# An attention + two-MoE kernel: finer pooling sums, a later load of the third batch, and the branch for further items moved between the two MoEs

## Chip, cores and metric

The kernel runs on one core of one Trainium2 chip. The metric is device time in microseconds (us): the median of the runs shown, lower is better. The profile is one more execution of the same program, with its own time.

## What is computed

```python
# attention: q, k, v are (8 batches, 8 heads, 576 rows, 64); K and V are pooled by 8 rows
k_p = k.reshape(B, H, Sp, pool, D).mean(axis=3)      # Sp = 72
v_p = v.reshape(B, H, Sp, pool, D).mean(axis=3)
attn = softmax(scale * q @ k_p.T)                    # 576 x 72 for each head
x = (attn @ v_p), heads side by side                 # 4608 tokens x 512
# first MoE: 8 experts (512 -> 1024 -> 512), each token goes to its best expert only
out[mask] = gate_w[mask, None] * (relu(x[mask] @ w1[e]) @ w2[e])
# second MoE: dense, three 512 -> 768 products, the largest of them, and back to 512
h = max(x @ w1, x @ w2, x @ w3)                      # elementwise
return h @ w_out                                     # 4608 x 512
```

All data are float32; products are made of high and low parts.

## The kernel before

The order of work on each engine is the order in which the code issues it; nothing reorders it. Three stretches follow each other.

**Attention (0 to about 160 us).** A loop over `it` runs 36 tiles of queries, and places beside them loads, pooling and the routing. SyncE (SP) loads: a batch's K and V come with `load_rows` (L193 for the rows of full 128-row chunks, L200 for a rest of 64 rows), a batch's queries with `load_q` (L215, tile `qgrp`). When K and V of batch `kvnext` are asked for is set by one condition in that loop, `kvnext * 4.5 - 11 <= it`; queries are asked for by `qorder` and `qneed`. In one turn of the loop the queries come first in the code, then K and V.

`prep_steps(b)` makes a batch's pooled K and V. For V always (`pool_v`), and for K from the third batch on (`pool_k2`), GpSimd (POOL) sums the 8 rows in three halvings, w = 4, 2 and 1: each `tensor_tensor` adds half of the rows to the other half in place (L267 for K, L280 for V), and the last one writes the pooled row to `kp` or `vp`. A batch has 576 pooled rows (8 heads of 72): four chunks of 128 partitions and one of 64. `spread_v` (L288) then sets V out by heads, also on POOL. VectorE (DVE) meanwhile takes maxima, subtracts (`sh`), normalises (L500 to L517), and works out the tokens' experts and their ranks in them (tiles `lg`, `oh`, `pre`, `im`; helpers at L547 and L551).

**First MoE (about 160 to 701 us).** Tokens are sorted by expert into items of 128. `run(range(NREQ), ...)` does the 22 items that are always needed (18 pairs of items and 4 single ones); the number of single items in fact needed is read from `nsing` (`values_load`, L1555) on all engines, when those 22 are issued. Results go to `ybuf` by SP (L1146). In gaps the weights of the second MoE are combined and written to `wdram` (L1169 to L1245).

**Second MoE (701 to 1246 us), `second`.** 6 groups of 768 tokens; in each, 9 chunks of weights (`wt`, 128x3584, loaded at L1585 into three buffers: the first three by POOL, all others by SP) go through `quad`: 42 matmuls each (L1617). The first 36 matmuls of the second MoE read the first chunk, `wt_0`, and the 37th reads `wt_1`. The products of seven sub-blocks are put together by ScalarE (ACT, `s`, L1625) and DVE (`blk`, `m`); then the output product (L1693), a copy by ACT with the gate (`ob`, L1699) and an indirect scatter to the output by POOL (`out_rows`, L1700). `tokens(g)` gathers the gates of a group (L1602, POOL). The rows of the first group are read from the first MoE's tiles while that MoE still runs.

**The branch.** Should more than 4 single items be needed, a branch (`tc.If(need > NREQ - NPAIR)`, L1757) after the second MoE runs them (`more`), two at a time, and does the last group of `second` once more, since such items hold tokens of that group. For these inputs it isn't taken. Every engine comes to it with its own compare-and-branch; an engine that skips it runs, at the end, instructions that bring the semaphores to where the skipped block would have left them, after a wait for its own earlier work (SP: for the DMAs of its queues, POOL: for those of its own, `INC_SWDGE_SEM` among them). The end of the program follows (L1798: drains and a barrier).

Of the kernel before, what the change touches and what calls it, by code (L numbers as in the profile page):

```python
# [8 lines left out]
F32 = mybir.dt.float32  # L9
# [5 lines left out]
A = mybir.AluOpType  # L15
AX = mybir.AxisListType.X
PSUM = bass.MemoryType.PSUM
# [4 lines left out]
def attention_moe_moe_kernel(  # L22
# [24 lines left out]
    nc = tc.nc  # L47
    dbg = dbg or {}

    P = 128  # L50
    B, H, S, D = q.shape
    N, DM = out.shape
    E, _, F = w1.shape
# [4 lines left out]
    DC = DM // P  # L58
# [4 lines left out]
    NPAIR = 18  # L63
    NSING = 8
    NB = 2 * NPAIR + NSING
    NITEM = NPAIR + NSING
    NREQ = NPAIR + NSING // 2
# [18 lines left out]
    GW = 768  # L86
    HW = GW // 2

    def pool(stack, name, bufs, side="left", space=None):
        kw = {"space": space} if space else {"side": side}  # L90
        return stack.enter_context(tc.tile_pool(name=name, bufs=bufs, reuse_waits="tile", **kw))
# [24 lines left out]
    if True:  # L116
# [61 lines left out]
        if True:  # L178
# [69 lines left out]
            def prep_steps(b):  # L248
# [14 lines left out]
                def pool_k2():  # L263
                    for c0, c1, n in ((0, 4, P), (4, 5, RC[4])):
                        for w in (4, 2, 1):
                            dst = kt[0:n, c0:c1, 0:w, :] if w > 1 else kp[0:n, c0:c1, 0:1, :]
                            nc.gpsimd.tensor_tensor(  # L267
                                dst, kt[0:n, c0:c1, 0:w, :], kt[0:n, c0:c1, w : 2 * w, :], op=A.add
                            )

                def dup_k():
                    for c0, c1, n in ((0, 3, P), (3, 4, KC[3]), (4, 5, KC[4])):
# [1 line left out]

                def pool_v(c0, c1, n):
                    for w in (4, 2, 1):
                        for a0 in range(c0, c1, 2) if w == 4 else (c0,):
                            a1 = min(a0 + 2, c1) if w == 4 else c1
                            dst = vt[0:n, a0:a1, 0:w, :] if w > 1 else vp[0:n, a0:a1, :].unsqueeze(2)
                            nc.gpsimd.tensor_tensor(  # L280
                                dst, vt[0:n, a0:a1, 0:w, :], vt[0:n, a0:a1, w : 2 * w, :], op=A.add
                            )
# [656 lines left out]
            def open_a(stack=left):  # L939

                tl["split"] = pool(stack, "wsplit", 3)
                tl["x"] = pool(stack, "xrow", 2)
# [25 lines left out]
            def load_w(i, piece):  # L968
                if i >= last[0]:
                    return  # L970
                if i >= NE:
                    finish_routing("slots")
                if piece == 0:
                    vals[i] = nc.sync.value_load(etab[0:1, i : i + 1], min_val=0, max_val=E - 1)
                e_ = bass.ds(vals[i], 1)
                if piece < 4:
                    src = w1[e_, :, 256 * piece : 256 * piece + 256].rearrange("o (c p) f -> p (o c) f", p=P)
                else:
                    src = w2[e_, 256 * (piece - 4) : 256 * (piece - 3), :].rearrange("o (c p) d -> p (o c) d", p=P)
                if i in (0, NREQ):  # L980
                    nc.sync.dma_start(w_raw(piece), src)
                else:
                    nc.sync.dma_start(w_raw(piece), src, cond=(vals[i] != vals[i - 1]), bounds_check="skip_entire_dma")
# [287 lines left out]
            def columns(g, whole_=True):  # L1271

                w_ = HW if whole_ else HW // 3
                at_ = [(c, n) for c in range(2) for n in range(0, HW, w_)]
                rows = []

                def load(k_):
                    if k_ < len(at_):
                        c, n = at_[k_]
                        t = tl["yr"].tile([P, 2, 2, w_], F32, tag="yr", name=f"yr{g}_{c}_{n}", bufs=2)
                        src = ybuf[:, GW * g : GW * g + GW].rearrange("(i c p) (j n) -> c p i j n", i=2, c=2, j=2)
                        for i in range(2):
                            nc.sync.dma_start(t[:, i], src[c, :, i, :, n : n + w_])
                        rows.append((t, c, n, w_))

                load(0)  # L1290
                load(1)
                for _ in range(1 if whole_ else 8):
                    yield
                for k_ in range(len(at_)):
                    yield from sums(*rows[k_])
                    load(k_ + 2)
# [180 lines left out]
            for it in range(NT + 4):  # L1477
                boundary()
                if it == MA:
                    skv.close()  # L1480
                    open_a()

                    for c in range(DC):
                        nc.gpsimd.dma_start(
                            ybuf[c * P : (c + 1) * P, N - (NITEM - NREQ) * P : N].rearrange("p (a n) -> p a n", n=P),
                            ones.unsqueeze(1).to_broadcast([P, NITEM - NREQ, P]),
                        )
                if it == NT:
                    sq_.close()
                    open_b()  # L1490
                while qnext < len(qorder) and qorder[qnext][0] * 9 + qneed[qorder[qnext][1]] - 4 <= it:
                    load_q(*qorder[qnext])
                    qnext += 1
                while kvnext < B and kvnext * 4.5 - 11 <= it:
                    kv[kvnext] = (load_rows("kraw", k, kvnext, KC if kvnext < 2 else RC), load_rows("vraw", v, kvnext, RC))
                    kvnext += 1
                if 0 <= it - 1 < NT:
                    stage_s(it - 1)
                if 0 <= it - 3 < NT:
                    stage_a(it - 3)  # L1500
                if it < NT:
                    stage_q(it)
                if 0 <= it - 1 < NT:
                    stage_e(it - 1)
                while squares:
                    squares.pop()()
                if it >= NT + 2:
                    next(first)
                if dense[0] == 2 and it < NT:
                    boundary()  # L1510
                if 0 <= it - 4 < NT:
                    stage_x(it - 4)
                if it == NT + 1:
                    next(first)
                for job in todo.get(it, []):
                    if callable(job):
                        job()
                        continue
                    b, j = job
                    if b not in cur:  # L1520
                        cur[b] = prep_steps(b)
                    cur[b][j]()
                if it == NT - 1 and started:
                    next(first)
                    next(first)
                if it == NT:
                    next(first)
                if it == NT + 3 or it - 3 in [t1 for _, t1 in CHK]:
                    while squares:
                        squares.pop()()  # L1530
                for m, (_, t1) in enumerate(CHK[:-1]):
                    if it - 4 == t1 - 1 and t1 < NT1:
                        queue.append([chain(rank_steps(m), slot_steps(nc.gpsimd))])
                    elif it - 4 == t1 - 1:
                        queue.append([chain(rank_steps(m), early_steps())])
                        dense[0] = 2
# [16 lines left out]
        for _ in cb:  # L1553
            pass
        need = nc.values_load(nsing[0:1, 0:1], min_val=0, max_val=NSING)  # L1555
    left.close()


# [6 lines left out]
    GB = GW // P  # L1565
    CH = F2C // 2 * 3

    def second(st, groups, again=False):
        wq = pool(st, "wstream", 3)
        yp = pool(st, "yin", 2)  # L1570
        t2 = pool(st, "tmp2", 2)
# [137 lines left out]
        for k_ in range(3):  # L1709
            load_chunk(k_)  # L1710
        tokens(groups[0])
        ahead = columns(groups[0]) if again else iter(())
        for g in groups:
            for _ in ahead:
                pass
# [23 lines left out]

    with ExitStack() as st:  # L1740
        second(st, list(range(NG)))

    def more(i0):

        last[0] = i0 + 2
        for p_ in range(8):
            load_w(i0, p_)
        gather(i0)
        for _ in run(range(i0, i0 + 2), lambda half, p_: None):
            pass  # L1750
        if i0 + 2 < NITEM:
            with tc.If(need > i0 + 2 - NPAIR):
                more(i0 + 2)


    assert (NITEM - NREQ) * P <= GW
    with tc.If(need > NREQ - NPAIR):  # L1757
        with ExitStack() as st:
            pq = pool(st, "pq2", 2, space=PSUM)
            pb = pool(st, "pb2", 1, space=PSUM)  # L1760
            wp1 = pool(st, "w1again", 1)
            tl["w1"] = [wp1.tile([P, DC, 256], F32, name=f"w1again{i}") for i in range(4)]
            tl.pop("py")
            open_a(st)
            open_c(st)
            more(NREQ)
        with ExitStack() as st:
            second(st, [NG - 1], True)


# [32 lines left out]
```

## Time and profile before

| | us |
|---|---|
| median of 3 runs | 1263.38 (1262.02 to 1263.81) |
| the profiled execution | 1260.98 |
| its span, first to last instruction | 1259.2 |
| PE busy in the span | 1215.6 (97%) |
| DVE busy | 799.2 (63%) |
| ACT busy | 580.5 (46%) |
| POOL busy | 318.9 (25%) |
| mean granted clock of TensorE | 0.991 of full speed |

The profiled execution lies 2.4 us below the median. A sum of changes is made on it and then set on the median. A line of a timeline reads: start, duration, engine, line, operation, out<-in, and in brackets how long the engine had been idle and what ended it. Lines of a source view read: line, engine, operation, count, durations in ns (minimum, median, maximum), first and last start in us. "SPq", "POOLq", "PEldq" are the sequencers of these engines (branches, semaphores, DMA issues).

### The profile page before, as it was taken

To read this page: it belongs to the slowest core of one execution; us is meant where nothing else is said; L and a number is where in the kernel's file an instruction comes from. 1 tells how busy PE (TensorE), PEld (TensorE's weight loads), DVE (VectorE), ACT (ScalarE), POOL (GpSimd) and SP (SyncE) were. 2 spreads that over 40 slices of the span, in tenths; PEclk is the share of its full clock that TensorE was granted. 3 is DMA by queue.
4 is the path that set the end of the run, shared out by engine and by line. 5 is a ranking of instruction groups with operands and counts; after the bars stand their busy time and mean duration, and the time that the engine had idled before them with its cause. 6 is when DMAs were issued, how large, how long until landed. Compare 5 with 4: busy or idle time off the path is not lost. (4 is left out here: it accounts for less than half of the span.)

```text
span 1259.2 us, 22318 instructions
## 1 busy us (share of the span) xinstructions
PE 1215.6 (97%) x8251; PEld 1158.0 (92%) x8251; DVE 799.2 (63%) x1575; ACT 580.5 (46%) x1040; POOL 318.9 (25%) x383
## 2 busy tenths in 40 slices
PE   5899899999999999999999999999999999999995
PEld 4788789999999999999999998998998998998994
DVE  6676886797889999898764446345445454454450
ACT  3466465545666676666655333323223323223221
POOL 6985553420212212222000302103103004004001
PEclk9899999999999999999999999999999999999998
DMA  9968246423976445844619666475564673773721
GB/s 252 267 202 236 97 138 217 151 85 32 298 262 226 164 143 203 283 151 137 207 51 350 241 238 242 160 262 205 207 239 182 220 264 153 258 263 124 253 108 52
DMA packets 98038, 246.21 MB, mean 196 GB/s; under 512 B 17100, under 2 KB 58106, under 8 KB 89858
## 3 DMA queue, kind: packets, MB, share of 16 engines
q1 hardware_dynamic: 84770, 189.09, 44.5%
q0 software_dynamic: 13152, 55.62, 13.3%
q8 instruction: 67, 1.10, 0.4%
q14 instruction: 49, 0.40, 0.1%
HBM read 252.23 MB, written 46.98 MB: 238 GB/s over the span
## 5 line engine op out<-in xcount | busy, mean ns | idle before, releaser
L1617 PE MATMUL p<-yhi,wt 128*128 128x384 f32 x1512 | 387.2, 336 | 0.0
L1617 PEld LDWEIGHTS p<-yhi,wt 128*128 128x128 f32 x1512 | 273.4, 188 | 0.6
L1617 PE MATMUL p<-ylo,wt 128*128 128x384 f32 x756 | 254.0, 336 | 0.0
L1625 ACT COPY s<-p 128x384 f32<-128x384 f32 x162 | 77.8, 480 | 221.1 <-PE p L1617 216.8
L1104 PE MATMUL py<-hhi,whi 128*128 128x256 f32 x576 | 164.6, 286 | 0.0
L1104 PE MATMUL py<-hhi,wlo 128*128 128x256 f32 x576 | 163.1, 283 | 1.6 <-DVE wlo L1036 1.6
L1056 PE MATMUL ph<-xhi,whi 128*128 128x256 f32 x576 | 163.8, 284 | 0.7 <-DVE hlo L1072 0.7
L1056 PE MATMUL ph<-xhi,wlo 128*128 128x256 f32 x576 | 163.0, 283 | 0.7 <-DVE wlo L1036 0.7
L1056 PE MATMUL ph<-xlo,whi 128*128 128x256 f32 x576 | 163.0, 283 | 0.0
L1104 PE MATMUL py<-hlo,whi 128*128 128x256 f32 x576 | 162.9, 283 | 0.0
L1617 PEld LDWEIGHTS p<-ylo,wt 128*128 128x128 f32 x756 | 142.1, 188 | 0.5
L1646 DVE TENSOR_TENSOR blk<-p,s 128x384 f32<-128x384 f32 x108 | 59.7, 553 | 113.9 <-PE p L1617 113.9
L1602 POOL DMA_INDIRECT gt<-gbuf,ix x26 | 37.0, 1424 | 312.1 <-DMA ix<-idbuf 305.7
L1104 PEld LDWEIGHTS py<-hhi,wlo 128*128 128x128 f32 x576 | 110.4, 192 | 1.8 <-DVE wlo L1036 1.8
L1056 PEld LDWEIGHTS ph<-xhi,whi 128*128 128x128 f32 x576 | 110.5, 192 | 1.2 <-DVE hlo L1072 0.9
L1056 PEld LDWEIGHTS ph<-xhi,wlo 128*128 128x128 f32 x576 | 110.5, 192 | 0.9 <-DVE wlo L1036 0.9
L1056 PEld LDWEIGHTS ph<-xlo,whi 128*128 128x128 f32 x576 | 110.5, 192 | 0.0
L1104 PEld LDWEIGHTS py<-hlo,whi 128*128 128x128 f32 x576 | 110.5, 192 | 0.0
L1104 PEld LDWEIGHTS py<-hhi,whi 128*128 128x128 f32 x576 | 110.4, 192 | 0.0
L1036 DVE TENSOR_TENSOR wlo<-w2raw,whi 128x1024 fp32r<-128x1024 f32 x84 | 102.2, 1221 | 8.8 <-ACT whi L1034 8.7
L1036 DVE TENSOR_TENSOR wlo<-w1raw,whi 128x1024 fp32r<-128x1024 f32 x67 | 81.8, 1220 | 27.6 <-ACT whi L1034 26.5
L1034 ACT CAST whi<-w2raw 128x1024 fp32r<-128x1024 f32 x88 | 91.8, 1044 | 7.7 <-PE py L1104 4.7
(316 smaller groups left out, 2280.8 us busy)
## 6 DMA issues: line engine op xcount, KB each, us to landing
wt<-wdram SPq DMA_DIRECT2D x51, 1792.0 KB
w1raw<-in_moe_w_dram SPq DMA_DIRECT2D x88, 512.0 KB
w2raw<-in_moe_w_dram SPq DMA_DIRECT2D x88, 512.0 KB
wdram<-wst POOLq DMA_DIRECT2D x9, 1792.0 KB
ybuf<-yo SPq DMA_DIRECT2D x40, 256.0 KB
cvraw<-in_moe_w_dram POOLq DMA_DIRECT2D x36, 256.0 KB
vraw<-in_v_dram SPq DMA_DIRECT2D x8, 1024.0 KB
xbuf<-x SPq DMA_DIRECT2D x16, 512.0 KB
```

The source lines that it names most:

```text
L1034: nc.scalar.copy(hi, src)
L1036: eng.tensor_tensor(lo, src, hi.bitcast(F32), op=A.subtract)
L1056: nc.tensor.matmul(ps[:, f, :], a_[:, c, fs], b_[:, c, :], start=(n == 0), stop=(n == 3 * DC - 1))
L1104: nc.tensor.matmul(py[:, c // 2, (c % 2) * 256 : (c % 2 + 1) * 256], a_[:, f, c * P : (c + 1) * P], b_[:, f, :], start=(piece == 0 and f = ...
L1602: nc.gpsimd.indirect_dma_start(out=gt[g][:, j : j + 1], out_offset=None, in_=gbuf[:, :], in_offset=bass.IndirectOffsetOnAxis(ap=cols[j], a ...
L1617: nc.tensor.matmul(ps, a_, b_, start=(start and c + n == 0), stop=(c == 1 and n == 2), skip_group_check=True)
L1625: nc.scalar.copy(t, ps)
L1646: tt(src, add[0], add[1], op=A.add)
```

## The change

Three edits. Line numbers after the first of them shift by up to 18: L1555 becomes L1557, L1585 becomes L1603, L1602 becomes L1620, L1617 becomes L1635.

```diff
 def pool_k2():
     for c0, c1, n in ((0, 4, P), (4, 5, RC[4])):
         for w in (4, 2, 1):
-            dst = kt[0:n, c0:c1, 0:w, :] if w > 1 else kp[0:n, c0:c1, 0:1, :]
-            nc.gpsimd.tensor_tensor(
-                dst, kt[0:n, c0:c1, 0:w, :], kt[0:n, c0:c1, w : 2 * w, :], op=A.add
-            )
+            for a0 in range(c0, c1, 4 // w):
+                a1 = min(a0 + 4 // w, c1)
+                dst = kt[0:n, a0:a1, 0:w, :] if w > 1 else kp[0:n, a0:a1, 0:1, :]
+                nc.gpsimd.tensor_tensor(
+                    dst, kt[0:n, a0:a1, 0:w, :], kt[0:n, a0:a1, w : 2 * w, :], op=A.add
+                )
...
 def pool_v(c0, c1, n):
     for w in (4, 2, 1):
-        for a0 in range(c0, c1, 2) if w == 4 else (c0,):
-            a1 = min(a0 + 2, c1) if w == 4 else c1
+        for a0 in range(c0, c1, 4 // w):
+            a1 = min(a0 + 4 // w, c1)
...
-                while kvnext < B and kvnext * 4.5 - 11 <= it:
+                while kvnext < B and max(kvnext * 4.5 - 11, kvnext - 1) <= it:
...
         need = nc.values_load(nsing[0:1, 0:1], min_val=0, max_val=NSING)
+
+        def more(i0):
+
+            last[0] = i0 + 2
+            for p_ in range(8):
+                load_w(i0, p_)
+            gather(i0)
+            for _ in run(range(i0, i0 + 2), lambda half, p_: None):
+                pass
+            if i0 + 2 < NITEM:
+                with tc.If(need > i0 + 2 - NPAIR):
+                    more(i0 + 2)
+
+
+        with tc.If(need > NREQ - NPAIR):
+            more(NREQ)
     left.close()
...
-    def second(st, groups, again=False):
+    def second(st, groups):
...
-        ahead = columns(groups[0]) if again else iter(())
+        ahead = iter(())
...
     with ExitStack() as st:
         second(st, list(range(NG)))
 
-    def more(i0):
...
-    with tc.If(need > NREQ - NPAIR):
-        with ExitStack() as st:
...
-            more(NREQ)
-        with ExitStack() as st:
-            second(st, [NG - 1], True)
```

**POOL, the pooling of K and V of the third batch.** Names ending in a number are tiles; a shape is the output's, `x4` is a count of equal rows. Before:

```order
L267 TENSOR_TENSOR kraw_254<-kraw_254 128x4x256
L267 TENSOR_TENSOR kraw_254<-kraw_254 128x4x128
L267 TENSOR_TENSOR kp_484<-kraw_254 128x4x64
L267 TENSOR_TENSOR kraw_254<-kraw_254 64x256
L267 TENSOR_TENSOR kraw_254<-kraw_254 64x128
L267 TENSOR_TENSOR kp_484<-kraw_254 64x64
L280 TENSOR_TENSOR vraw_257<-vraw_257 128x2x256 x2
L280 TENSOR_TENSOR vraw_257<-vraw_257 128x4x128
L280 TENSOR_TENSOR kp_484<-vraw_257 128x4x64
```

Now:

```order
L269 TENSOR_TENSOR kraw_287<-kraw_287 128x256 x4
L269 TENSOR_TENSOR kraw_287<-kraw_287 128x2x128 x2
L269 TENSOR_TENSOR kp_490<-kraw_287 128x4x64
L269 TENSOR_TENSOR kraw_287<-kraw_287 64x256
L269 TENSOR_TENSOR kraw_287<-kraw_287 64x128
L269 TENSOR_TENSOR kp_490<-kraw_287 64x64
L282 TENSOR_TENSOR vraw_290<-vraw_290 128x256 x4
L282 TENSOR_TENSOR vraw_290<-vraw_290 128x2x128 x2
L282 TENSOR_TENSOR kp_490<-vraw_290 128x4x64
```

Every sum over 128 partitions now covers 256 elements of each. The first sum with w = 2 reads what the first two sums with w = 4 wrote, with two more of these between; before, it read what the instruction right before it wrote. The two first batches change in V alone.

**SP, the loads after V of the second batch (`vraw_251`, now `vraw_254`).** Before:

```order
L193 DMA kraw_254<-in_k_dram 128x4x512
L200 DMA kraw_254<-in_k_dram 64x512
L193 DMA vraw_257<-in_v_dram 128x4x512
L200 DMA vraw_257<-in_v_dram 64x512
L215 DMA qgrp_2_288<-in_q_dram 128x8x256
```

Now:

```order
L215 DMA qgrp_2_285<-in_q_dram 128x8x256
L193 DMA kraw_287<-in_k_dram 128x4x512
L200 DMA kraw_287<-in_k_dram 64x512
L193 DMA vraw_290<-in_v_dram 128x4x512
L200 DMA vraw_290<-in_v_dram 64x512
```

One load of queries goes ahead of the third batch's K and V; all later batches keep their places.

**POOL, between the MoEs.** In brackets: the semaphores of a row's wait (DMAHW: SP's DMAs, DMASW: POOL's own). Before, from the read of `nsing`:

```order
L1555 TENSOR_LOAD nsing [waits DVE_49]
L1585 DMA wt_0_9369<-wdram_63 128x3584 [waits DMAHW4_49,DMAHW5_49,DMAHW3_49,DMAHW6_49,DMAHW2_49,DMAHW7_49,DMAHW1_49,DMAHW0_49]
L1585 DMA wt_1_9371<-wdram_64 128x3584 [waits DMAHW3_49,DMAHW6_49,DMAHW1_49,PE_49]
L1585 DMA wt_2_9373<-wdram_65 128x3584
```

Now, from the end of the skipped block (the branch itself, L1572, stands right behind the read of `nsing`):

```order
L1568 UNCONDITIONAL_BRANCH
L1572 ISA [waits DMASW6_49,DMASW7_49,DMASW1_49,DMASW0_49]
L1572 UNCONDITIONAL_BRANCH
L1603 DMA wt_0_9987<-wdram_63 128x3584 [waits DMAHW4_49,DMAHW3_49,DMAHW5_49,DMAHW2_49,DMAHW6_49,DMAHW1_49,DMAHW7_49,DMAHW0_49,DMASW6_49]
L1603 DMA wt_1_9989<-wdram_64 128x3584 [waits DMAHW4_49,DMAHW3_49,DMAHW5_49,DMAHW1_49,DMAHW6_49,DMAHW0_49,DMAHW7_49,DMASW7_49,PE_49]
L1603 DMA wt_2_9991<-wdram_65 128x3584 [waits DMASW0_49]
```

The load of `wt_1` waited for three of SP's DMA semaphores and now waits for seven, at values that SP reaches only when it has skipped the block; for `wt_0` the values are ones that SP reaches before it. PE's first matmul of the second MoE follows the branch on its engine, and waits for ACT's skip too:

```order
L1128 MATMUL pyT_9939<-ident,yr_9937 128x128 x4
L1568 UNCONDITIONAL_BRANCH x2
L1572 UNCONDITIONAL_BRANCH
L1635 MATMUL p_0_0_10012<-yhi_8110,wt_0_9987 128x384
L1635 MATMUL p_0_0_10012<-ylo_8111,wt_0_9987 128x384
```

Before, the first `p` matmul (L1617) stood right behind `pyT` and PE's read of `nsing`. At the end of the program POOL's last rows of before, `L1757` branches and an `ISA`, are gone: the end (L1789, before L1798) follows the last scatter.

## Rows read from the trace of the kernel before

**Rows 1.** Page, busy time, share of the span and instructions of each engine.
```profile
PE 1215.6 (97%) x8251; PEld 1158.0 (92%) x8251; DVE 799.2 (63%) x1575; ACT 580.5 (46%) x1040; POOL 318.9 (25%) x383
```

**Rows 2.** Waits of PE, 16 to 150 us: total, times, longest.
```profile
PE pav L490 <- DVE dt L515: 4.6, 2, 3.2
...
PE psc L436 <- DVE pre L547: 2.4, 1, 2.4
```

**Rows 3.** Windows: length, busy of PE, PEld, DVE, ACT, POOL, then clock, DMA share, GB/s.
```profile
40.00:45.00 5.00, 4.31 (x20) 3.63 (x21) 1.47 (x4) 1.99 (x5) 4.76 (x6) 0.69 1.08 281
45.00:50.00 5.00, 5.00 (x26) 4.69 (x24) 2.26 (x5) 2.22 (x5) 4.76 (x6) 0.63 1.07 340
...
130.00:140.00 10.00, 6.84 (x41) 5.99 (x40) 10.00 (x11) 2.52 (x6) 9.61 (x12) 0.83 0.10 34
```

**Rows 4.** Timeline, POOL and DVE, around 35 us and 131 us.
```profile
33.76 4.04 DVE L551 TENSOR_SCALAR im<-iof 128x10 f32<-128x10 f32 x1
...
35.42 3.69 POOL L267 TENSOR_TENSOR kraw<-kraw 128x1024 f32<-128x1024 f32 x2
...
41.48 3.83 POOL L280 TENSOR_TENSOR vraw<-vraw 128x512 f32<-128x512 f32 x3
...
129.57 3.92 DVE L547 TENSOR_TENSOR oh<-w,wm 128x72 f32<-128x72 f32 x1
...
131.06 3.67 POOL L267 TENSOR_TENSOR kraw<-kraw 128x1024 f32<-128x1024 f32 x2
```

**Rows 5.** POOL by line and shape, 0 to 160 us: count, busy us, mean ns.
```profile
L267 POOL TENSOR_TENSOR kraw<-kraw 128x1024 f32<-128x1024 f32 x6 | 14.1, 2351 | 0.0
...
L267 POOL TENSOR_TENSOR kp<-kraw 128x256 f32<-128x256 f32 x6 | 4.4, 730 | 0.7 <-PE ptk L313 0.4
```

**Rows 6.** Timeline, SP and PE, the queries of tile `qgrp`.
```profile
23.59 0.59 SPq L215 DMA_DIRECT2D qgrp<-in_q_dram  x1
...
40.69 0.63 PE L411 MATMUL pqT<-ident,qgrp 128*128 128x128 f32 x4 [2.88 <-DMA qgrp<-in_q_dram]
```

**Rows 7.** Timeline, POOL, between the MoEs.
```profile
658.53 0.58 POOL L1585 DMA_DIRECT2D wt<-wdram  x1
...
695.45 1.08 POOL L1585 DMA_DIRECT2D wt<-wdram  x2 [36.34 <-DMA ybuf<-yo]
...
707.29 1.00 POOL L1602 DMA_INDIRECT gt<-gbuf,idg  x1 [1.30 <-DMA wt<-wdram]
```

**Rows 8.** Timeline, PE, ACT and SP, where the second MoE begins.
```profile
700.79 0.66 PE L1126 MATMUL pyT<-ident,yr 128*128 128x128 f32 x4 [0.68 <-ACT yr L1097]
...
701.33 0.41 PE L1617 MATMUL p<-yhi,wt 128*128 128x384 f32 x1
...
701.48 0.59 ACT L1128 COPY yo<-pyT 128x512 f32<-128x512 f32 x1 [0.74 <-PE pyT L1126]
...
701.76 0.51 PE L1617 MATMUL p<-yhi,wt 128*128 128x384 f32 x2
702.09 0.39 SPq L1146 DMA_DIRECT2D ybuf<-yo  x1
...
702.29 0.51 PE L1617 MATMUL p<-yhi,wt 128*128 128x384 f32 x2
```

**Rows 9.** DMA of 690 to 712 us in 40 slices of 0.55 us, GB/s.
```profile
GB/s 382 377 310 156 76 47 21 5 0 0 0 15 235 182 235 443 417 469 417 417 417 417 443 391 443 469 417 417 426 111 304 86 0 0 1 0 0 31 0 131
```

**Rows 10.** Source view of the branch of before, at the end of the program.
```profile
L1757 SPq EVENT_SEMAPHORE  x9: 17/17/17, 1207.7 to 1208.7; - x9
...
L1757 SPq COMPARE_BRANCH  x1: 53/53/53, 1201.4 to 1201.4; - x1
L1757 DVEq COMPARE_BRANCH  x1: 72/72/72, 1224.8 to 1224.8; - x1
L1757 DVEq EVENT_SEMAPHORE  x1: 21/21/21, 1225.4 to 1225.4; - x1
L1757 PEldq COMPARE_BRANCH  x1: 3372/3372/3372, 1241.6 to 1241.6; - x1
...
L1757 POOLq INC_SWDGE_SEM  x1: 1810/1810/1810, 1249.9 to 1249.9; - x1
```

**Rows 11.** Timeline, POOL, the last scatter.
```profile
1247.03 0.98 POOL L1700 DMA_INDIRECT out_dram<-ob,ix  x1 [2.99 <-ACTq L1757]
```

**Rows 12.** Source view of L1798, the program's end.
```profile
L1798 POOLq DRAIN  x3: 46/109/6689, 1251.7 to 1258.9; - x3
```

More of the change, by code (lines that the diff above doesn't have):

```diff
@@ L1741, in attention_moe_moe_kernel @@
         second(st, list(range(NG)))
-    def more(i0):
[L1745 to L1756, printed above, removed]
-    with tc.If(need > NREQ - NPAIR):
-        with ExitStack() as st:
[L1759 to L1765, printed above, removed]
-            more(NREQ)
-        with ExitStack() as st:
-            second(st, [NG - 1], True)
 _INS = [
```

## The prediction, made before the changed kernel was run

> **What bounds the kernel now.** I read the page first: PE is busy 97% of the span, ACT and DVE about half of it or somewhat more, POOL a quarter [rows 1]. So the time is PE's stream of matmuls, plus the places where that stream stands still or runs at the lower clock, plus the tail after it. Whatever the change does must show in one of these three, and I went to each place that it touches.
>
> In the attention, the waits of PE show that its two long ones behind DVE end at `dt` and `pre` [rows 2]. Both are small DVE operations that wait for POOL. The timeline shows how: `oh`, 72 elements, takes 3.92 us, from 129.57 to about 133.4, and POOL's first K sum runs from 131.06 and takes 2.35 us [rows 4, 5], that is, to 133.4. `im`, 10 elements, takes 4.04 us, from 33.76 to 37.80, and the K sum that starts at 35.42 ends at 37.77. So DVE did not get in where one POOL instruction followed another at once, but where a sum had to wait for the one right before it. The windows add the price behind a wait: after PE's pauses the granted clock is 0.69 and 0.63 over 40 to 50 us and 0.83 over 130 to 140 us; 5 x 0.31 + 5 x 0.37 = 3.4 us are lost in the first of these, 1.7 us in the second [rows 3].
>
> Between the MoEs PE runs on without a wait: `pyT` at 700.79, then the first `p` matmul at 701.33 [rows 8]. At the end, the last scatter is issued at 1247.03 [rows 11], POOL's `INC_SWDGE_SEM` starts at 1249.9 [rows 10] and a drain of 6.69 us at 1251.7 [rows 12].
>
> **The change, part by part.**
>
> *Finer sums.* A sum of 256 elements takes 0.73 us alone [rows 5]; back to back I reckon 0.69. With w = 4 and 2 a batch's K then takes (4 + 2) x 0.69 = 4.14 instead of 3.69 us, its V 4.14 instead of 3.83 [rows 4]: POOL works 0.3 us longer for each of the first two batches, 0.75 for each of six others. Only in the opening does PE wait on a sum itself: +0.3. The rest lies beside PE's work, and POOL's pooling isn't late elsewhere. But the stretch in which DVE is held changes. Before, a gap came after the first K sum, 2.35 us after the start. Now the first sum with w = 2 needs a result two instructions back, so the first gap comes where w = 1 waits for w = 2, after 4.14 us. `oh` would get in at 131.06 + 4.14 = 135.2 instead of 133.4: +1.8 us, and PE, which waits 3.2 us there for the `dt` queued behind `oh` on DVE, waits longer by as much. The pause that ends at `pre` is held by V in the same way, 2.5 us to the first gap before, 4.14 now: +1.6. Some of it comes back, since the later gaps lie closer together, and POOL's added work shifts which DVE operation meets which sum. I take +2 for both with the opening's 0.3. The bounds: if every boundary now lets DVE in, the pauses at `dt` and `pre` go (3.2 + 2.4) with the 1.7 of clock behind the first, -7; if both are fully lengthened and another lock arises, +5.
>
> The Trainium skill ("SBUF — State Buffer", section on who interferes with whom) calls the port pair that DVE and GpSimd share an exclusive lock; read as one lock for each instruction, shorter instructions would let DVE in sooner, and the sum would be negative here. The rows above agree with the lock and speak against release at each boundary: `oh` was queued before 131.06, when POOL's spread ended and K began, and did not get in there.
>
> *Later load of the third batch.* The queries `qgrp` were issued at 23.59 behind K and V of that batch, and PE waited 2.88 us for them, to 40.69 [rows 6]. They now go first, and land earlier by the 2.36 MB that went ahead of them, 7 us or more at 281 to 340 GB/s [rows 3]; that wait goes. What is late next is DVE: `im` would be held to 35.42 + 4.14 = 39.56 instead of 37.80, and the softmax chain behind it on DVE, on which PE's next products stand, slips by 1.8 us. K of that batch lands some 4 us later, which POOL, on V and spreads until 35.4, just covers. I take 0; the bounds are +1.5 and -6.3 (all of 2.88, and 3.4 of clock).
>
> *The branch between the MoEs.* Its code is skipped, but each engine brings its semaphores up after its own work, and POOL's load of `wt_1` now waits for SP's skip. Before, `wt_1` was issued at 695.45 [rows 7], and the first 36 matmuls, 0.52 us for three [rows 8], ended at 701.33 + 6.25 = 707.6, where `wt_1` is first read. Now: SP issues the last `ybuf` store at 702.09, 0.39 us long [rows 8]; it lands about 2 us later (the last scatter: issue ends at 1248.0, landed by 1249.9 [rows 10, 11]), at 704.4. Until then SP reads `nsing` and jumps. Jumps cost, from compare to first semaphore, 0.6 us on DVE, 3.37 on PE for the compare alone, and 6.3 on SP (1201.4 to 1207.7), with nine semaphores over 1.0 us behind it [rows 10]. SP's was behind a chunk of 1.8 MB then in flight and would not be now; I take 2 us from 703.4, so semaphores from 705.4 to 706.1. `wt_1` is issued there. Its flight: both chunks were issued at 695.45 and landed at 707.29, where a gather that waits for them goes [rows 7]; one chunk of 1.835 MB takes 4.3 us at the 430 GB/s shown [rows 9], so the first landed near 703, 7.5 us after its issue. 706.1 + 7.5 = 713.6 against 707.6: **+6.0**. PE's own start (ACT's skip, a jump like the 3.37) moves quad 0 to 702.7 to 705, which this wait hides: 705 + 6.25 = 711.3. `wt_2` and six gathers queue behind `wt_1` on POOL; `wt_2` is needed a quad (7.3 us) later and lands 4.3 later, so it adds nothing. Bounds: +4 (no cost of SP's jump beyond the store, a flight of 6.5) and +10 (a jump of 6.3); 2 us to 3.4 more if the pause drops the clock as it did at 41 and 134 us.
>
> The Trainium skill ("Runtime: NRT & Kernel Launch", section on instruction fetch mechanics) says that a taken branch whose target lies outside the window of loaded pages stalls until the target's page is fetched. PE's 3.37 us agree, DVE's 0.6 us do not show such a stall; by the rule alone, SP's jump would be nearer PE's, and the sum 1.4 us higher.
>
> *The end.* The branches, the wait for the last scatter's landing and `INC_SWDGE_SEM` (1.81 us) go. If the drain of 6.69 us then starts where the last issue ends, 1248.0 instead of 1251.7, the end comes 3.7 us sooner: **-3.7**. Bounds: 0 (the drain is itself the wait for something that ends at its own time), -1.8 (it counts from the landing) and -8 (it only followed from `INC_SWDGE_SEM`, and shrinks as well, to leave only the landing).
>
> **Sum:** +2 + 0 + 6.0 - 3.7 = +4.3 us. On the profiled 1260.98 that is 1265.3; on the median of 1263.38, which I forecast, 1267.7, rounded to **1267**.
>
> **Rivals.**
>
> *A. DVE gets in (faster).* If the finer sums free DVE at each boundary, the pauses behind `oh`, `pre` and `im` and for `qgrp` go: up to -7 and -6.3; half of it, -6.5, with +6.0 and -3.7 gives -4, about 1259; all of it 1253. It decides once the opening and attention give back more than the 2.3 us that the middle and the end leave. For it: each of these pauses is a real pause of PE, and no row of before shows sums as short as these back to back at 128 partitions. Against: the boundaries of equal instructions in rows 4. Chance 0.22.
>
> *B. The end gives more than assumed (faster or even).* The drain shrinks: -8 against +6 and 0 to +2: 1261 to 1263.5. For it: the two other drains take 0.05 and 0.11 us [rows 12]. Against: nothing shows what the long one waits for. Chance 0.13.
>
> *C. Middle and end cancel (even).* SP's jump is hidden by the store and the wait is +4, the attention moves by less than 1: about 1264. Chance 0.15.
>
> *D. Worse.* SP's jump costs 6 us or the clock falls behind the new pause: +9 in the middle, +7 in sum: 1271. Chance 0.15.
>
> The forecast itself has 0.35. That the change doesn't do what it says is no rival: the order shows each row moved, and the branch stays not taken.
>
> **Numbers.** A measurement of this kernel tells about 0.2%, 2.5 us, from no change: faster means under 1260.9, slower over 1265.9. Faster: A's larger part 0.17 and 0.07 of B, with 0.04 from C and the forecast's edge: 0.28. Same: the rest of B, most of C and a part of A and the forecast: 0.22. Slower: 0.50. Range: 1256 (A without its extreme) to 1273 (D with some of the attention's upper bound); the forecast's own cases alone lie at 1264 to 1270.
>
> **What would show it.** `wt_1` issued about 706 and PE waiting for it near 711 to 713, with a `DMA wt<-wdram` wait of 2 to 5 us; no `INC_SWDGE_SEM` at the end and the long drain from 1248 relative to the last scatter; `oh` longer than 3.9 us, `im` longer than 4.0; no `qgrp` wait at 40 us. It is wrong if `wt_1` goes out before 703, if DVE's small operations under POOL's sums fall to under 1.5 us and PE's pauses at 37, 89 and 130 us shrink, or if the drain vanishes.

## The result, and the profile after

The changed kernel takes **1281.82 us** (median; 1280.39 to 1283.68), the kernel before in the same runs 1263.6: ratio 1.0141, 95% interval 1.0118 to 1.0164, 15 to 21 us slower. Forecast: slower, to 1267, in 1256 to 1273. The direction was right, the size was not: the time lies above the range. The profiled execution took 1282.09 us, its span is 1280.4.

I followed PE through both traces: it issues the same 8251 matmuls in the same order, so each can be set against its counterpart. On the clock of the kernel before, the changed kernel's lag is -0.3 us at 25 us, +5.8 at 37, back to +0.7 at 48, +5.7 at 94, +12.1 at 140, +11.3 at 155; +11.1 at 677 and +13.0 at 679; +17.4 at the first matmul of the second MoE, +24 ten microseconds later, and +24.1 at the last. The end gives 2.9 back. So there are two losses, some 11 us in the attention and 11 to 13 between the MoEs. One trace stands for one execution: the profiled execution of the kernel before lies 2.4 us below its median, and the attention of before, profiled again in e3, e4, e7 and e12 (below), ends at 160 us between 1.4 us ahead of this trace and 2.5 behind it. The 11 us are far outside that; single waits are not always.

**The attention.** PE's waits of the changed kernel, over the whole run (total, times, longest):

```profile
PE pav L492 <- DVE dt L517: 8.9, 2, 5.5
PE psc L424 <- DVE sh L456: 4.4, 1, 4.4
PE p L1635 <- PEq L1572: 4.2, 1, 4.2
PE p L1635 <- DMA wt<-wdram: 2.5, 1, 2.5
...
PE ph L1066 <- DMA w1raw<-in_moe_w_dram: 1.5, 2, 0.8
```

The wait for `qgrp` [rows 6] is gone, and PE waits 4.4 us for `sh`. Neither is the change's doing alone: in the profiles of e3, e4, e7 and e12, with the loads and sums of before, PE doesn't wait for `qgrp` either, and in e3 and e4 it waits 3.5 and 3.1 us for `sh`. e3's row:

```profile
PE psc L422 <- DVE sh L454: 3.5, 1, 3.5
```

So the wait for `qgrp` belongs to one execution of the kernel before. What is new are the waits at `dt`, 8.9 us where they were 4.6 [rows 2], and 5.8 at most in those four. What holds them stands in the timeline of DVE and POOL around 35 us, 87 us and 140 us:

```profile
32.63 5.63 DVE L553 TENSOR_SCALAR thq<-iof 128x13 f32<-128x13 f32 x1
...
87.02 3.70 DVE L549 TENSOR_TENSOR oh<-w,wm 128x72 f32<-128x72 f32 x1
...
136.03 5.70 DVE L549 TENSOR_TENSOR oh<-w,wm 128x72 f32<-128x72 f32 x1
...
143.81 4.42 DVE L549 TENSOR_TENSOR pre<-pre 128x72 f32<-128x72 f32 x1
```
```profile
32.11 2.04 POOL L290 TENSOR_TENSOR vbd<-vp,mslot 128x128 f32<-128x128 f32 x5
34.11 4.12 POOL L269 TENSOR_TENSOR kraw<-kraw 128x256 f32<-128x256 f32 x6
...
137.53 4.12 POOL L269 TENSOR_TENSOR kraw<-kraw 128x256 f32<-128x256 f32 x6
```

`thq`, 13 elements, is issued under POOL's five spreads and ends at 38.26, just after the six sums have ended at 38.23; `oh` ends at 141.73, the six sums at 141.65. Before, `oh` took 3.92 us [rows 4], and `pre`, in the same place, 2.62. Near 87 us, too, an operation had been held before, for 2.75 us. These two rows are of the kernel before:

```profile
85.76 2.75 DVE L617 COPY pre<-oh 128x72 f32<-128x72 f32 x1
...
137.08 2.62 DVE L547 TENSOR_TENSOR pre<-pre 128x72 f32<-128x72 f32 x1
```

Nine boundaries of POOL instructions passed without letting `thq` in. Not every DVE operation is held: in the changed kernel a TENSOR_REDUCE of `kraw` that began at 30.02, under two of POOL's sums, took 1.06 us, against 1.02 with POOL idle (26.07 in the kernel before). The windows then show the clock (length, PE, PEld, DVE, ACT, POOL, clock, DMA share, GB/s):

```profile
95.00:100.00 5.00, 5.00 (x26) 4.93 (x25) 2.17 (x7) 1.32 (x5) 0.00 (x0) 0.56 0.82 224
140.00:145.00 5.00, 2.98 (x10) 2.58 (x10) 5.00 (x7) 0.00 (x0) 4.77 (x9) 0.53 0.00 0
145.00:150.00 5.00, 3.75 (x17) 3.48 (x17) 4.97 (x7) 1.07 (x2) 4.84 (x8) 0.50 0.00 0
150.00:155.00 5.00, 5.00 (x25) 4.69 (x23) 2.69 (x7) 2.66 (x8) 0.46 (x2) 0.60 0.27 108
720.00:725.00 5.00, 5.00 (x19) 5.00 (x19) 0.00 (x0) 1.43 (x3) 2.11 (x3) 0.60 0.29 59
```

After PE's pause near 90 us the granted clock falls to its lower level (0.50 of full, 1.2 GHz), which it did not do in the trace of before, but did in e3's and e12's (0.68 and 0.55 from 90 to 95 us). From 140 to 155 us it is there almost throughout; before, 130 to 140 us had 0.83 [rows 3] and the next 5 us 1.00. Over 16 to 160 us, before, after and in e1 (the sums alone):

```profile
16.00:160.00 144.00, 129.08 (x917) 114.76 (x918) 104.76 (x248) 79.33 (x201) 106.56 (x141) 0.95 0.70 208
16.00:160.00 144.00, 123.69 (x834) 110.58 (x834) 107.22 (x223) 71.92 (x181) 108.83 (x184) 0.91 0.66 199
16.00:160.00 144.00, 125.40 (x828) 112.38 (x828) 106.06 (x222) 70.85 (x179) 107.91 (x183) 0.87 0.66 199
```

In e3, e4, e7 and e12 the mean clock was 0.93 to 0.96. PE's waits from 16 to 160 us grew by about 5 us, from 15 to 20; the other 6 us of the lag arise in matmuls, and I put them down to the clock. That split is read from single traces; no run takes the clock alone.

**Between the MoEs.** Timeline of POOL, PE and SP, and the branch by source (L1572):

```profile
713.81 0.66 PE L1128 MATMUL pyT<-ident,yr 128*128 128x128 f32 x4 [0.68 <-ACT yr L1099]
...
715.11 0.38 SPq L1148 DMA_DIRECT2D ybuf<-yo  x1
...
718.70 0.66 PE L1635 MATMUL p<-yhi,wt 128*128 128x384 f32 x1 [4.23 <-PEq L1572]
...
722.59 1.08 POOL L1603 DMA_DIRECT2D wt<-wdram  x2 [49.71 <-issue]
...
730.06 0.42 PE L1635 MATMUL p<-yhi,wt 128*128 128x384 f32 x1 [2.45 <-DMA wt<-wdram]
```

```profile
L1572 SPq EVENT_SEMAPHORE  x9: 17/17/17, 716.9 to 719.7; - x9
...
L1572 POOLq INC_SWDGE_SEM  x1: 2253/2253/2253, 669.2 to 669.2; - x1
...
L1572 PEldq COMPARE_BRANCH  x1: 3972/3972/3972, 714.4 to 714.4; - x1
...
L1572 SPq COMPARE_BRANCH  x1: 53/53/53, 716.3 to 716.3; - x1
```

PE jumps for 3.97 us and stands still for 4.23; the clock then falls (0.60 above), so the first 36 matmuls, up to 727.6, take 8.9 us where they took 6.3; `wt_1` comes 2.45 us too late, and the clock falls again. SP's nine semaphores stretch over 2.8 us, since one waits, as I read it, for the landing of the `ybuf` store. SP is through at 719.7, but POOL issues `wt_1` only at 722.59.

**The end.** The last scatter and the drains:

```profile
1271.83 0.98 POOL L1718 DMA_INDIRECT out_dram<-ob,ix  x1 [2.70 <-DMA out_dram<-ob,ix]
```
```profile
L1789 POOLq DRAIN  x3: 46/115/7908, 1271.6 to 1280.1; - x3
```

The long drain ends at 1279.5, 6.7 us after the last issue ends (1271.83 + 0.98); before it took 6.69 from the end of `INC_SWDGE_SEM` [rows 12]. From the start of PE's last matmul to the end it is 10.7 us instead of 13.6.

### The profile page after: what moved, and what is told of

It reads as the page before. It is cut to its first block, busy times and chain, and to the rows that moved or that the text cites. A ratio compares the mean times of both kernels' runs of the same rounds, so it can differ in the third digit from the quotient of the medians.

```text
span 1280.4 us, 22375 instructions
## 1 busy us (share of the span) xinstructions
PE 1225.9 (96%) x8251; PEld 1167.5 (91%) x8251; DVE 809.4 (63%) x1575; ACT 580.7 (45%) x1040; POOL 325.2 (25%) x431
## 5 line engine op out<-in xcount | busy, mean ns | idle before, releaser
L1635 PE MATMUL p<-yhi,wt 128*128 128x384 f32 x1512 | 390.4, 338 | 6.7 <-PEq L1572 4.2
L1635 PEld LDWEIGHTS p<-yhi,wt 128*128 128x128 f32 x1512 | 276.1, 190 | 7.7 <-issue 7.2
L1635 PE MATMUL p<-ylo,wt 128*128 128x384 f32 x756 | 255.8, 338 | 0.0
L1635 PEld LDWEIGHTS p<-ylo,wt 128*128 128x128 f32 x756 | 143.4, 190 | 0.5
L1620 POOL DMA_INDIRECT gt<-gbuf,ix x26 | 38.9, 1495 | 309.5 <-DMA ix<-idbuf 303.1
L1656 DVE TENSOR_TENSOR m<-p,s 128x384 f32<-128x384 f32 x54 | 30.1, 558 | 103.2 <-PE p L1635 103.0
```

Source lines behind the costliest of these rows:

```text
L1620: nc.gpsimd.indirect_dma_start(out=gt[g][:, j : j + 1], out_offset=None, in_=gbuf[:, :], in_offset=bass.IndirectOffsetOnAxis(ap=cols[j], a ...
L1635: nc.tensor.matmul(ps, a_, b_, start=(start and c + n == 0), stop=(c == 1 and n == 2), skip_group_check=True)
L1656: tt(mx[key], add[0], add[1], op=A.add)
```

## The experiments

My theory after this: the sums lengthen the stretch in which POOL's instructions follow one another without one that waits for the one before, DVE is held out for all of it, and the clock falls behind the longer pauses; the branch costs its jump, the clock, and a late `wt_1`. The rivals are named with each run. A ratio is to the kernel before, in the same set of runs.

| run | median us | ratio | 95% interval |
|---|---|---|---|
| e1: the sums alone | 1273.27 | 1.0069 | 1.0045 to 1.0092 |
| e2: the load alone | 1264.54 | 1.0014 | 0.9994 to 1.0035 |
| e3: the branch alone | 1271.47 | 1.0055 | 1.0038 to 1.0072 |
| e4: no branch anywhere | 1258.04 | 0.9955 | 0.9936 to 0.9973 |
| e5: the same sums, another order | 1261.32 | 0.9984 | 0.9973 to 0.9995 |
| e6: sums by halves | 1257.87 | 0.9956 | 0.9937 to 0.9975 |
| e7: the branch alone, short block | 1269.38 | 1.0063 | 1.0042 to 1.0084 |
| e8: e5 and the load | 1260.31 | 0.9980 | 0.9967 to 0.9993 |
| e9: e6 and the load | 1260.21 | 0.9981 | 0.9967 to 0.9995 |
| e10: the change with e6's sums | 1268.26 | 1.0039 | 1.0023 to 1.0056 |
| e11: e6 again | 1258.37 | 0.9969 | 0.9957 to 0.9981 |
| e12: e3, `wt_1` and `wt_2` by SP | 1266.19 | 1.0032 | 1.0018 to 1.0046 |

### The three parts (e1, e2, e3)

Each takes one of the three edits of the diff alone: e1 the two loops of `pool_k2` and `pool_v`, e2 the condition of the load, e3 the branch.

> Before with the finer sums alone. Theory (sums that run one behind another without a dependency hold DVE out for 4.1 us instead of 2.4): slower by 8 to 13 us, all of it before 160 us; the long DVE operations are oh and thq at 3.5 to 6 us, and the granted clock falls behind PE's pauses near 90 and 140 us. Rival (the later load shifts POOL against DVE, and the sums only add their own 0.3 to 0.75 us a batch): slower by under 3 us.

> Before with the later load of the third batch alone. Theory: PE's 2.9 us wait for qgrp goes, and with the sums as before little takes its place: faster by 1 to 4 us, no clock below 0.9 from 40 to 50 us if the pause goes entirely. Rival (the load shifts POOL's K and with it the locks): slower by 3 us or more.

> Before with the branch between the MoEs alone. Theory: the middle costs 9 to 12 us (PE's jump 4, two falls of the clock 2 each, the wait for wt_1 2 to 3, a later wt_0 beside weight loads 1 to 2), the end gives back 3: slower by 6 to 9 us. Rival (the change's middle loss is mostly the attention's delay carried on): slower by under 4 us.

By the ratios the sums cost 8.7 us, the load 1.8 (not told from nothing), the branch 6.9: together 17.4, and the whole change measured 17.8. The parts add up, each to within 2 or 3 us. Each landed where the theory for it put it but the load, which gained nothing. e1's timeline of DVE shows the holds of the whole change again:

```profile
32.18 5.70 DVE L553 TENSOR_SCALAR thq<-iof 128x13 f32<-128x13 f32 x1
...
137.33 5.70 DVE L549 TENSOR_TENSOR oh<-w,wm 128x72 f32<-128x72 f32 x1
...
145.10 4.42 DVE L549 TENSOR_TENSOR pre<-pre 128x72 f32<-128x72 f32 x1
```

In e2 PE takes the queries at once, and a DVE operation that had been free is caught later, under five spreads and the first K sum (78.34 + 2.35 = 80.69); one row of PE, DVE and POOL each:

```profile
37.79 0.60 PE L411 MATMUL pqT<-ident,qgrp 128*128 128x128 f32 x4
```
```profile
76.11 4.61 DVE L551 TENSOR_SCALAR lg<-lg,rtau 128x72 f32<-128x72 f32 x1
```
```profile
78.34 3.68 POOL L267 TENSOR_TENSOR kraw<-kraw 128x1024 f32<-128x1024 f32 x2
```

e2's PE is 4.5 us ahead at 47 us, 2.2 ahead at 84 and level at 94. Not all of that is the load's: e3, e4, e7 and e12, with the load of before, are 0.1 to 2.5 us ahead of the same trace at 47 us. The rest was given back where PE and DVE had moved against POOL's sums: the DVE operations longer than 2.4 us in the attention add up to 17.8 us in e2, 13.3 before, and `lg` is the difference.

### The end (e4)

The branch and its block at the end of the program are deleted.

> Before without any branch for further items (left out: those items, of which these inputs have none). Theory (the long drain starts when the last scatter is issued, not after INC_SWDGE_SEM): faster by 3 to 4 us, all of it after the last matmul. Rival (the drain ends at its own time): within 1 us of before.

In the profile 3.5 us: the span is 1255.7 instead of 1259.2, with PE's last matmul at the same time to 0.15 us. The runs say 3.4 to 8.1. Its drains, by source:

```profile
L1771 POOLq DRAIN  x3: 46/115/7910, 1246.9 to 1255.4; - x3
```

As in the changed kernel, the drain stands behind the last scatter (1247.17 to 1248.15) and ends 6.7 us after it. That it ends at its own time is ruled out.

### The order of the sums (e5), and sums by halves (e6, e11)

e5 has the instructions of the finer sums, in another order; e6 has sums of 512, 256 and 128 elements, one half of the batch after the other. In both, the loops over w and a0 become `for w, a0, a1 in sums(c0, c1)`:

```diff
# e5: in pool_k2 and pool_v, each sum adds w rows of chunks a0 to a1
+def sums(c0, c1):
+    for h0 in range(c0, c1, 2):
+        for a0 in range(h0, min(h0 + 2, c1)):
+            yield 4, a0, a0 + 1
+        yield 2, h0, min(h0 + 2, c1)
+    yield 1, c0, c1
# e6
+def sums(c0, c1):
+    for h0 in range(c0, c1, 2):
+        for w in (4, 2, 1):
+            yield w, h0, min(h0 + 2, c1)
```

> Before with the finer sums of the change, the same instructions in another order: w = 4 of two chunks, then w = 2 of these, so that a sum waits for the one right before it after at most three sums (2.1 us; in the change six, 4.1 us). Theory (DVE gets in only where a sum waits for its predecessor): at least 6 of the 8.7 us of the sums come back, to 1258 to 1266; oh and im hold at most 2.2 us after a sum begins. Rival (it is the number of POOL instructions, or POOL's longer time): as slow as the sums in the change's order, 1270 to 1275.

> Before with the sums by halves of a batch, each half down to w = 1 before the next: sums of 512, 256 and 128 elements, each but the first of a half waiting for the one before. At most 1.8 us without such a wait, 0.8 to 1.2 us more of POOL's time a batch. Theory: faster than before by 1 to 5 us. Rival (POOL's time counts): slower than before by 2 us or more.

> The sums by halves once more, with more rounds: whether its 1257.9 stands. Theory: 1257 to 1260, its interval below the kernel before; rival (the first result was a lucky phase of the locks): 1260 to 1263.

e5 against e1 is the run that decides: the same sums with the same sizes, and 12 us between them (10.7 by the ratios). Neither the number of POOL's instructions nor its time (115 us busy from 16 to 160 in e5, 108 in e1) can be the loss. The DVE operations longer than 2.4 us in the attention add up to 22.0 us in e1 (five of them), 21.9 in the changed kernel, 13.3 before, 10.8 in e5 (three), 9.2 and 6.9 in e6 and e11, which are one kernel: among the kernels with the branch at the end, the times go in the same order. The longest hold in e5 near 130 us:

```profile
129.38 3.67 DVE L622 COPY pre<-oh 128x72 f32<-128x72 f32 x1
```
```profile
129.58 2.04 POOL L293 TENSOR_TENSOR vbd<-kp,mslot 128x128 f32<-128x128 f32 x5
131.59 2.88 POOL L274 TENSOR_TENSOR kraw<-kraw 128x256 f32<-128x256 f32 x4
```

It is held through five spreads and two sums (131.59 + 1.4 = 133.0) and gets in where the third, with w = 2, waits for the second. I had expected at most 2.2 us after the sums begin, and that holds (1.5). What is left of the holds is mostly the spreads, which don't depend on one another.

All fourteen traces together bear the rule out for long holds. In their attention, 88 of the routing's DVE operations took over 1 us under POOL's sums and spreads; every one got in where POOL paused between two of these (0.08 us, or more, where one waits), and they passed 249 boundaries without a pause. Short holds show an exception: right behind such a pause DVE also got in after one sum, with the next following at once (before: `pre` from 134.89 to 135.63, POOL's `kp` from 134.81 to 135.54).

e6 is the fastest complete version of the study, confirmed by e11: 4 to 5 us below the kernel before in both sets, though its sums take POOL longer than those of before (112 and 114 us busy from 16 to 160, against 107).

The Trainium skill ("SBUF — State Buffer", on who interferes with whom) calls the shared port pair an exclusive lock. The holds agree with a lock. Shorter instructions alone don't open it (e1); an instruction that waits for the one before it does (e5). How it passes from one engine to the other at a boundary no run shows.

### The load with better sums (e8, e9), and the change with better sums (e10)

> Before with the sums in the order of e5 and the later load of the third batch; the branch stays at the end. Theory: the 4.6 us that the load gave until 80 us and that the locks took back later are kept in part: 1255 to 1262, faster than the order alone by 1 to 4 us. Rival (the load only shifts where DVE meets a sum): within 2 us of the order alone.

> Before with the sums by halves and the later load of the third batch; the branch stays at the end. Theory: with short stretches the wait for qgrp that the load takes away isn't given back whole: 1254 to 1259, at or below the halves alone (1257.9). Rival (the load only shifts where DVE meets a sum): 1258 to 1262.

> The changed kernel with its sums by halves in place of its own. Theory (the parts add up; the branch's 7 us are left, the sums' 9 us go and 3 to 5 more): 1263 to 1269. Rival (middle and attention depend on each other): above 1272.

e8 is 1 us below e5, inside its rival's bounds and on the edge of the theory's; e9 at 1260.2 is no better than e6, and its runs spread from 1254.58 to 1262.98. The load is worth nothing that can be told in any company. e10 lies 13.6 us below the changed kernel by the medians, about what the change's sums cost (8.7) and the halves gain (4 to 5) together, and still 4.9 above the kernel before: the sums were most of the loss in the attention, and the branch's loss stays.

### The middle (e7, e12)

e7 shortens the skipped block to one item (`last[0] = i0 + 1`, `range(i0, i0 + 1)`, no inner branch). e12 is e3 with one number changed:

```diff
-                eng = nc.gpsimd if k_ < 3 else nc.sync
+                eng = nc.gpsimd if k_ < 1 else nc.sync
```

> The branch between the MoEs alone, with a block of one item (left out: items beyond the fifth single one, of which these inputs have none), a quarter of the code that is skipped. Theory: PE's compare-and-branch falls from 4.0 us to under 1, but wt_1 still goes out only after SP's skip, so that PE waits longer for it: faster than the full block by 0 to 3 us (only a fall of the clock can go). Rival (PE's jump is the loss of the middle): faster than the full block by 4 us or more. Rival (the jump does not go by the length): PE's jump stays at 4 us.

> The branch between the MoEs alone, with wt_1 and wt_2 loaded by SP instead of POOL. With the branch alone POOL issued wt_1 2.9 us after the last of its waits that the trace shows. Theory (that time is POOL's own, on its way to a DMA): SP issues wt_1 within 1 us of its skip, and the kernel is 1.5 to 3.5 us faster than the branch alone, 1268 to 1270. Rival (a semaphore not seen holds the load): SP issues it as late, 1271 to 1273.

e7, the branch by source and PE's wait:

```profile
L1567 PEldq COMPARE_BRANCH  x1: 352/352/352, 701.9 to 701.9; - x1
```
```profile
PE p L1630 <- DMA wt<-wdram: 7.2, 1, 7.2
```

PE's jump falls from 3.41 us in e3 to 0.35, and PE waits 7.2 us for `wt_1` instead of 2.4. By the medians 2.1 us come back, though the ratios, from different sets, don't tell e7 from e3. The traces show none of it in the middle: between 677 and 712 us PE falls 12.5 us behind in e3 and 12.4 in e7. The jump is hidden by the wait for `wt_1`, as the theory had it. The Trainium skill ("Runtime: NRT & Kernel Launch", on instruction fetch mechanics) says that a taken branch out of the loaded pages waits for its target to be fetched; a jump of 3.41 us over four items (256 matmuls) and of 0.35 over one agrees.

In e3, SP's nine semaphores and POOL's load of `wt_1`:

```profile
L1570 SPq EVENT_SEMAPHORE  x9: 17/17/17, 709.3 to 711.9; - x9
```
```profile
714.84 1.08 POOL L1601 DMA_DIRECT2D wt<-wdram  x2 [49.36 <-PE p L1633]
```

In e12, SP's nine semaphores and its loads, and PE's waits:

```profile
L1570 SPq EVENT_SEMAPHORE  x9: 17/17/17, 706.2 to 708.8; - x9
```
```profile
709.07 10.86 SPq L1601 DMA_DIRECT2D wt<-wdram  x3
```
```profile
PE p L1633 <- PEq L1570: 3.6, 1, 3.6
PE pyT L1126 <- ACT yr L1097: 0.7, 1, 0.7
```

SP issues `wt_1` 0.3 us after its last semaphore; POOL took 2.9 in e3 (711.9 to 714.84). PE's wait for `wt_1` is gone, only the jump is left, and 5.3 us come back by the medians, 2.9 by the ratios. I had expected 1.5 to 3.5. The traces side with the larger figure: PE falls 7.3 us behind in the middle where e3 has 12.5, and 4 of these 5 us are the wait for `wt_1` with the second fall of the clock behind it. So the delay is POOL's own, and in e12 POOL's first gather has it instead (3.1 us, 708.84 to 711.95); why it has it the traces don't say.

## Why the prediction went wrong

**The branch: right mechanism, mis-sized term.** "`wt_1` is issued there" (706.1) and "+6.0". With the -3.7 of the end that made +2.3; e3 measured +6.9. That PE's own start would hide in the wait for `wt_1` was right (e7). Three sizes were off: the `ybuf` store landed 3.3 us after its issue in e7 (702.6 to 705.9), not 2.3; POOL took 2.9 us to issue `wt_1` (e3), where SP took 0.3 (e12); and the clock fell twice, which I had in the bounds and not in the sum. With 1 to 2 us at weight loads near 679 us, which all kernels with the branch in the middle show, e3's trace has 12.5 us between 677 and 712. They stand where `wt_0` is issued later, behind POOL's `INC_SWDGE_SEM`, but no run took that alone. SP's jump cost 0.5 us (716.3 to 716.9), not the 2 that I took.

**The sums: the step that failed.** "I take +2 for both"; measured 8.7 (5.7 to 11.6). The mechanism was right, and both holds that I priced came out: `oh` longer by 1.8 (3.92 to 5.70), `pre` by 1.8 where I had 1.6 (2.62 to 4.42). Three things were wrong with the term. "Some of it comes back, since the later gaps lie closer together" did not show: from 129 to 155 us PE's lag grew by 5.6 us, against 1.5 to 1.7 in e3, e4, e7 and e12. The holds near 82 and 87 us, in the routing's first chain, had no term at all, without a reason: `lg` went from 0.67 to 2.45 us, a hold of 2.75 became one of 3.70, and PE lost 5.3 us between 80 and 94 (0 to 2.3 in those four). And I priced PE's pauses without what follows them: after the longer pauses the matmuls ran at the lower clock, by my reading about half of the loss. I had read that price in the windows [rows 3] and used it only for a gain.

**The load: right in size, in part by luck.** "I take 0": e2 is within the noise. But the gain that I set against the loss, the 2.88 us of `qgrp`, was a wait of one execution: of the later profiles that keep the load of before (e1, e3 to e7, e11, e12) none has it. And the place where e2 gives its lead back was wrong: not at `im` but some 35 us later (`lg`, 4.61 us).

**The end: right.** -3.7 forecast, -2.9 in the changed kernel's trace, -3.5 in e4's; in the changed kernel the last scatter also waits for the one before it to land. The rival B, in which the drain shrinks, fell.

**The rivals.** C (middle and end cancel) fell with e3. A (DVE gets in at every boundary) fell with e1; the argument against it, from rows 4, was the right one, and should have cost it more than half of its 0.22. D had the right sign of every term and still lay 11 us too low, since it raised one term at a time. The terms share a part: behind a longer pause of PE the clock fell in the middle as in the attention, and the upper end of the range had to raise them together. The sum of 1267.7 was also written down as 1267, not 1268, which changes nothing.

## What to carry to other kernels

Where POOL and DVE share a stretch of time, look at which POOL instruction waits for its predecessor: a DVE operation that meets a long run of POOL's without such a wait is held to its end, so the order of the sums can be worth more than their size. Before a wait in a trace gets a price, see whether a second execution has it too: the 2.88 us for `qgrp` did not come back. A branch over code that is not run is not free: price the jump by the length of the block, each engine's wait for its own work, and every load whose semaphores only the skip brings up, and let the engine issue that load whose skip ends last. Price a pause of TensorE together with the time that it spends at the lower clock behind it.

## What the runs showed of the hardware that I had not expected

- A DVE operation of 13 elements was held for 5.63 us, over nine boundaries between POOL's instructions (the changed kernel).
- POOL issued a DMA 2.9 us after the last semaphore that it waited for, after a pause of some 50 us (e3; likewise after 49.7 us in the changed kernel), SP 0.3 us after its own (e12).
- PE's jump over 256 matmuls took 3.41 us (e3) to 3.97 (the changed kernel), over a quarter of them 0.35 (e7).
- The drain at the program's end ends 6.7 us after POOL's last DMA issue, in the changed kernel and in e4.
